# Attention and a maxout MLP as one hand-ordered pipeline over units of two chunks

## The chip, the cores and the metric

The kernel runs on one core of one Trainium2 chip. The metric is device microseconds of one execution. A core has a matrix engine (PE, with weight loads shown apart as PEld), a vector engine (DVE), an activation engine (ACT), GpSimd (POOL), and SyncE (SP), whose queue here issues all transfers between device memory (DRAM) and the on-chip memory (SBUF). Matmul results land in the accumulators (PSUM), which DVE and ACT read.

## The reference

The inputs r, k, v, w have the shape [4 batches, 8 heads, 768 positions, 48]; w is a decay between 0.8 and 0.95. For each batch and head a 48x48 state runs over the positions, and its outputs, put together over the heads, are 3072 tokens of 384 features for a maxout MLP:

```
for t in range(S):
    cur = u * k[t] outer v[t]
    y[t] = r[t] @ (state + cur)
    state = w[t][:, None] * state + k[t] outer v[t]
x = y as [3072 tokens, 384]
out = np.maximum(x @ w1, x @ w2) @ w_out        # w1, w2: [384, 1024], w_out: [1024, 384]
```

The result is f32.

## The kernel before, in words

Positions are cut into chunks of 128, so that a batch has 6 chunks and the whole has 24, taken batch by batch (L98 to L188). For a chunk the decays are summed as logarithms: `lw` is the logarithm of w (ACT, L116), a matmul with a triangle of ones gives the sum over the earlier positions, `excl_p` (L118), and two exponentials give the factors by which r and k are scaled (`Aexcl`, `Ainv`). The scaled `rp` and `kp` are transposed head by head on PE, 48 columns each (L153, L154), and copied out of PSUM by DVE (`rT`, `kT`). Scores `mt_p` are one matmul a head (L163), are masked by DVE (`MTm`, L164), and give `y_p` with v (L168) and with the state of the chunk before (L171). The term with u is a DVE reduction (`diag`) times v. The state `S_new` gets k transposed times v (L180) and is scaled by the decay of the whole chunk, `Wtot_b`: eight matmuls a chunk against a column of ones (L141) put the sum of `lw` over the chunk onto the partitions that hold the state's rows, and ACT takes the exponential (L143). All chunk outputs go to `x_sb`, which stays on chip.

The MLP starts when the attention has ended, in 6 blocks of 512 tokens. max(a, b) is taken as (a + b + |a - b|) / 2: `wd_sb` is w1 - w2, `gT` is the absolute value of x @ wd (L210, L212), and the half that is linear in x is one matmul with `wc_sb` = (w1 + w2) @ w_out, made before the attention (L82 to L91). Tokens are transposed to feature-major `xT` (L204, L205); the result `op` is feature-major too (L216, L219), is copied (L222), transposed back on PE (L225), copied by DVE (L227) and stored in 64 KB pieces (L229).

Every engine works through its instructions in order. The order is set by the framework's scheduler, which takes the program as written and moves instructions of each engine ahead by its own costs; waits between engines are semaphores that the framework puts in. A tile of a pool with one buffer (all PSUM tiles but `mt_p`) is written again only when its last reader is done.

## Time and profile before

| | before |
|---|---|
| three timed runs, median (lowest to highest) | 425.43 us (425.3 to 425.91) |
| profiled execution: its span, first to last instruction | 422.0 us |
| the same execution with what lies around the span, 3.4 us by the median of the timed runs | 425.4 us |
| attention with its preparation, up to about | 300 us |
| MLP, from about | 300 us to 422 us |
| busy: PE, DVE, ACT, POOL | 314.5, 244.0, 142.7, 2.7 us |
| mean granted TensorE clock | 0.687 of full speed |

How to read the views: a row of the groups has the source line, the engine, the operation, the tile written and the tiles read, shapes and count, then busy microseconds in total, the mean of one in nanoseconds, and the idle time of the engine just before with what ended it. A row of the timeline has the start, the duration from the first to the end of the last instruction of the row, the engine (SPq is the queue of SP: the time that it spends on issuing a transfer, not the transfer) and the instruction, with xN for N of a kind. A matmul with f32 operands is two instructions in every view. A matmul's own duration includes its way through the array; a row of several gives the spacing, which is what N of them cost in a stream. A row of the stages has start and end, length, busy time and count of each engine, the granted clock of TensorE (1.00 is full speed, 0.50 half), the mean busy share of the DMA engines, and GB/s.

### The profile page before, as it was taken

The page shows a single profiled execution, that of the slowest core. Times are in us where ns is not written, and L with a number is a line of the kernel's source. Part 1 is how long each engine was busy: PE and PEld are TensorE (multiplying, and loading weights), DVE is VectorE, ACT ScalarE, POOL GpSimd, SP SyncE. Part 2 cuts the span into 40 slices and gives each one's busy share as a digit, 9 for nine tenths or more (in the row PEclk, how much of TensorE's full clock was granted, in tenths as well). Part 3 has the DMA queues.
Part 4 walks back from the last instruction along what each step waited for, and adds up shares of the span by engine and source line. Part 5 has one row for each costly group of instructions (what it writes and reads, how often), then busy time and mean ns, then how long its engine had stood idle before and what let it go on. Part 6 is the DMA issues. An engine that isn't in the chain of part 4 may idle for free.

```text
span 422.0 us, 5555 instructions
## 1 busy us (share of the span) xinstructions
PE 314.5 (75%) x2078; PEld 189.2 (45%) x2088; DVE 244.0 (58%) x596; ACT 142.7 (34%) x206; POOL 2.7 (1%) x16
## 2 busy tenths in 40 slices
...
PEclk9998565555555555555555555555799999999997
...
DMA packets 112076, 28.67 MB, mean 68 GB/s; under 512 B 101041, under 2 KB 111282, under 8 KB 112050
## 3 DMA queue, kind: packets, MB, share of 16 engines
...
## 4 chain that ended last, share of the span: by engine, by line
PE 53%; DVE 18%; ACT 17%; DMA 6%; issue 5%; SPq 0%; ACTq 0%; DVEq 0%
PE g L210 9%; PE Wtot_p L141 7%; PE y_p L168 6%; ACT gT L212 6%; PE y_p L171 6%; PE op L216 5%; ACT L116 5%; PE tp_k L154 5%; DVE MTm L164 4%; PE mt_p L163 3%; DVE x_sb L175 3%; PE op L219 3%; PE tp_r L153 3%; DVE S_new L184 2%; DMA w2f<-in_moe_w_dram 2%
## 5 line engine op out<-in xcount | busy, mean ns | idle before, releaser
L118 PE MATMUL excl_p<-lw,triU 128*128 128x384 f32 x48 | 38.8, 910 | 34.2 <-DVE incl L122 33.5
L143 ACT ACTIVATE Wtot_b<-Wtot_p 48x384 f32<-48x384 f32 x24 | 11.6, 484 | 120.8 <-DVE S_new L184 119.6
L210 PE MATMUL g<-xT,wd_sb 128*128 128x512 bf16 x138 | 41.4, 391 | 13.5 <-ACT gT L212 12.4
L205 DVE COPY xT<-tp 128x128 bf16<-128x128 bf16 x72 | 16.1, 224 | 54.0 <-PE tp L204 54.0
L212 ACT ACTIVATE gT<-g 128x512 bf16<-128x512 f32 x48 | 28.7, 597 | 53.5 <-PE g L210 52.7
L216 PE MATMUL op<-gT,wo_sb 128*128 128x512 bf16 x140 | 41.6, 381 | 3.8 <-ACT gT L212 2.5
L227 DVE CAST osx<-tp 128x128 f32<-128x128 bf16 x72 | 20.8, 289 | 40.7 <-PE tp L225 27.6
L168 PE MATMUL y_p<-vb,MTm 128*128 128x48 bf16 x192 | 38.1, 220 | 5.7 <-DVE MTm L164 5.7
L141 PE MATMUL Wtot_p<-ones_col,lw 128*48 128x1 f32 x384 | 33.2, 216 | 5.2 <-ACT lw L116 3.5
L141 PEld LDWEIGHTS Wtot_p<-ones_col,lw 128*48 128x48 f32 x384 | 31.2, 186 | 10.5 <-ACT lw L116 7.8
L171 PE MATMUL y_p<-S_b_new,rT 48*128 48x48 bf16 x160 | 34.8, 218 | 0.0
L156 DVE COPY kT<-tp_k 48x512 bf16<-48x512 bf16 x48 | 19.9, 414 | 23.2 <-PE tp_k L154 23.1
L164 DVE TENSOR_TENSOR MTm<-mt_p,maskU 128x512 bf16<-128x512 f32 x48 | 31.0, 686 | 2.7 <-PE mt_p L163 0.2
L153 PE MATMUL tp_r<-ident,rp 128*48 128x128 bf16 x192 | 29.8, 308 | 2.8 <-DVE rp L127 2.5
L153 PEld LDWEIGHTS <-rp 128*48 128x48 bf16 x192 | 18.3, 145 | 26.9 <-DVE vb L131 16.2
L154 PE MATMUL tp_k<-ident,kp 128*48 128x128 bf16 x192 | 29.8, 309 | 0.7 <-DVE kT L156 0.4
L163 PE MATMUL mt_p<-rT,kT 48*128 48x128 bf16 x192 | 28.3, 302 | 0.5 <-DVE kT L156 0.5
L116 ACT ACT_TABLE_LOAD x22 | 28.2, 1283 | 1.1 <-PEq L248 0.7
L118 PEld LDWEIGHTS excl_p<-lw,triU 128*128 128x128 f32 x48 | 11.8, 305 | 37.0 <-DVE incl L122 35.8
L120 ACT ACT_TABLE_LOAD x22 | 28.2, 1283 | 0.4
L210 PEld LDWEIGHTS <-wd_sb 128*128 128x128 bf16 x144 | 13.9, 98 | 31.7 <-issue 22.8
L168 PEld LDWEIGHTS <-MTm 128*128 128x128 bf16 x192 | 18.4, 106 | 19.3 <-DVE MTm L164 12.5
...
## 6 DMA issues: line engine op xcount, KB each, us to landing
rt<-in_r_dram SPq DMA_DIRECT2D x24, 192.0 KB, 3.8
kt<-in_k_dram SPq DMA_DIRECT2D x24, 192.0 KB, 3.6
vt<-in_v_dram SPq DMA_DIRECT2D x24, 192.0 KB, 2.7
wt<-in_w_dram SPq DMA_DIRECT2D x24, 192.0 KB, 3.1
out_dram<-osx SPq DMA_DIRECT2D x72, 64.0 KB, 1.5
w1f<-in_moe_w_dram SPq DMA_DIRECT2D x1, 1536.0 KB, 6.4
w2f<-in_moe_w_dram SPq DMA_DIRECT2D x1, 1536.0 KB, 9.9
wof<-in_moe_w_out_dram SPq DMA_DIRECT2D x1, 1536.0 KB, 7.1
```

What stands on the lines that cost most here:

```text
L116: nc.scalar.activation(lw, wt, AF.Ln)
L118: nc.tensor.matmul(excl_p, triU, lw.rearrange("a b c -> a (b c)"))
L141: nc.tensor.matmul(Wtot_p[:, h:h + 1], lw[:, h, :], ones_col)
L153: nc.tensor.transpose(tp_r[:, j, :], rp[:, h, :], ident)
L154: nc.tensor.transpose(tp_k[:, j, :], kp[:, h, :], ident)
L163: nc.tensor.matmul(mt_p[:, j, :], kT[:, h, :], rT[:, h, :])
L164: nc.vector.tensor_mul(MTm[:, half * 4:half * 4 + 4, :], mt_p, maskU4)
L168: nc.tensor.matmul(y_p[:, h * D:(h + 1) * D], MTm[:, h, :], vb[:, h, :], start=True, stop=(c == 0))
L171: nc.tensor.matmul(y_p[:, h * D:(h + 1) * D], rT[:, h, :], S_b[:, h, :], start=False, stop=True)
L210: nc.tensor.matmul(g1, wd_sb[:, ko, fo * C:(fo + 1) * C], xT[:, ko, :], start=(ko == 0), stop=(ko == KO - 1))
L212: nc.scalar.activation(gT[:, fo, :], g1, AF.Abs)
L216: nc.tensor.matmul(op, wo_sb[:, fo, ko * C:(ko + 1) * C], gT[:, fo, :], start=(fo == 0), stop=False)
```

## The change

The function is written anew. The work is cut into 12 units; a unit is one chunk position of two batches (J = 2), so that units 2c and 2c + 1 hold chunk c of batches 0, 1 and 2, 3. The framework's scheduler is off (`manual_schedule`): each engine does its instructions in the order of the code. A loop of 14 steps takes in step n three units at different stages, interleaved piece by piece: unit a = n is prepared (decay sums `cs`, scaling `pre3`), unit t = n - 1 is in the attention proper (`tr`, `qk`, `kv`, `yy`, `decay`, and `xt`, the transpose of its outputs), and unit m = n - 2 is in the MLP (`gg`, `oo`).

Inside the pieces:

- Loads are 384 KB each, four a unit, issued two steps ahead. The MLP weights are loaded behind the inputs of units 0 and 1, and made ready (`weights`) in step 1.
- One table of ACT functions that holds both logarithm and exponential is loaded once.
- r and k of a head lie in 64 columns of which 16 are zero, so that one transpose takes two heads (8 transposes of 128 columns a chunk, for r and k together, where there were 16), and the second head's rows start at partition 64.
- The decay of a whole chunk comes from the last row of the inclusive sums `inc`: a transfer writes this row to DRAM, two transfers read it back one element at a time onto the partitions of the state (`WL`), and ACT takes the exponential (`Wt`). The matmuls against the column of ones are gone.
- The copy of v, the product with u, its product with v, and the state's scaling and copy go from DVE to POOL.
- The state's matmul and its use take two heads at once, with zero blocks beside the diagonal ones.
- The MLP's second product is token-major: `xT` and `gT` are the weights and `wo_sb`, `wc_sb` stream with 384 columns. The result is copied by ACT and stored, 192 KB a chunk, with no transpose back. The factor 0.5 sits in `wo_sb`, which ACT makes.
- PSUM tiles: one buffer each for `ex`, `tr`, `sc0`, `sc1`, `y`, `o`, two for `g`. `tr` serves `tr` and `xt`, `ex` serves `cs` and `kv`.

The diff, added lines only; the lines it takes away are the kernel above:

```diff
+    with tc.manual_schedule(), nc.allow_non_contiguous_dma(reason="one row moved onto partitions"):
+        _body(tc, r, k, v, w, u, moe_w1, moe_w2, moe_w_out, out)
...
+    NP = H // 2
+    J = 2
+    DP = 64
+    NU = NC * B // J
+    nc.scalar.preload_act_table_set("natural_log_exp_and_others")
     const = tc.alloc_tile_pool(name="cst", bufs=1)
+    ldp = tc.alloc_tile_pool(name="ld", bufs=4)
+    wk = tc.alloc_tile_pool(name="wk", bufs=2)
+    drp = tc.alloc_tile_pool(name="dr", bufs=3, space=bass.MemoryType.DRAM)
+    ps = tc.alloc_tile_pool(name="ps", bufs=1, space=bass.MemoryType.PSUM)
+    def unit(u_):
+        return u_ // 2, (u_ % 2) * J
+    L = {}
+    def load(u_):
+        c, b0 = unit(u_)
+        sl = bass.ds(c * C, C)
+        d = {}
+        for name, src in (("w", w), ("k", k), ("r", r), ("v", v)):
+            t = ldp.tile([C, J, H, D], F32, tag="l" + name, name="l" + name)
+            nc.sync.dma_start(
+                out=t.rearrange("s b h d -> s (b h) d"),
+                in_=src[b0:b0 + J, :, sl, :].rearrange("b h s d -> s (b h) d"))
+            d[name] = t
+        L[u_] = d
+    load(0)
+    u_b = const.tile([C, HD], F32)
+    nc.sync.dma_start(out=u_b, in_=u.rearrange("h d -> (h d)").partition_broadcast(C))
+    load(1)
+    w1f = const.tile([C, KO, d_ff], F32)
+    w2f = const.tile([C, KO, d_ff], F32)
+    wof = const.tile([C, FO, HD], F32)
+    nc.sync.dma_start(out=w1f, in_=moe_w1.rearrange("(o p) n -> p o n", p=C))
+    nc.sync.dma_start(out=w2f, in_=moe_w2.rearrange("(o p) n -> p o n", p=C))
+    nc.sync.dma_start(out=wof, in_=moe_w_out.rearrange("(o p) n -> p o n", p=C))
...
+    def weights():
+        for ko in range(KO):
+            nc.vector.tensor_sub(wd_sb[:, ko, :], w1f[:, ko, :], w2f[:, ko, :])
+            nc.gpsimd.tensor_add(ws_sb[:, ko, :], w1f[:, ko, :], w2f[:, ko, :])
+        nc.scalar.mul(wo_sb, wof, 0.5)
...
+        for ko in range(KO):
+            wc_p = ps.tile([C, HD], F32, tag="o", name="o")
+            for fo in range(FO):
+                nc.tensor.matmul(wc_p, wsT_sb[:, fo, ko * C:(ko + 1) * C],
+                                 wo_sb[:, fo, :], start=(fo == 0), stop=(fo == FO - 1))
+            nc.scalar.copy(wc_sb[:, ko, :], wc_p)
+    U = {}
+    def pre1(n):
+        t = L[n]
+        s = {}
+        U[n] = s
+        s["lw"] = lw = wk.tile([C, J, H, D], F32, tag="lw", name="lw")
+        nc.scalar.activation(lw, t["w"], AF.Ln)
+        s["vb"] = vb = wk.tile([C, J, H, D], BF16, tag="vb", name="vb", bufs=3)
+        nc.gpsimd.tensor_copy(vb, t["v"])
+        rku = wk.tile([C, J, H, D], F32, tag="rku", name="rku", bufs=1)
+        nc.gpsimd.tensor_mul(rku, t["r"], t["k"])
+        nc.gpsimd.tensor_mul(
+            rku.rearrange("s j h d -> s j (h d)"), rku.rearrange("s j h d -> s j (h d)"),
+            u_b.unsqueeze(1).to_broadcast([C, J, HD]))
+        s["rku"] = rku
+        s["inc"] = wk.tile([C, J, HD], F32, tag="inc", name="inc")
+        s["A"] = wk.tile([C, J, H, D], F32, tag="A", name="A")
+    def pre1b(n):
+        s = U[n]
+        dg = wk.tile([C, J, H, 1], F32, tag="dg", name="dg")
+        nc.vector.reduce_sum(dg, s["rku"], axis=AX.X)
+        s["vd"] = vd = wk.tile([C, J, H, D], F32, tag="vd", name="vd", bufs=3)
+        nc.gpsimd.tensor_mul(vd, L[n]["v"], dg.to_broadcast([C, J, H, D]))
+    def cs(n, j):
+        s = U[n]
+        ex = ps.tile([C, HD], F32, tag="ex", name="ex")
+        nc.tensor.matmul(ex, triU, s["lw"][:, j].rearrange("s h d -> s (h d)"))
+        nc.scalar.activation(s["A"][:, j].rearrange("s h d -> s (h d)"), ex, AF.Exp)
+        nc.vector.tensor_add(s["inc"][:, j, :], ex, s["lw"][:, j].rearrange("s h d -> s (h d)"))
+    def pre3(n):
+        s = U[n]
+        iA = wk.tile([C, J, H, D], F32, tag="iA", name="iA", bufs=1)
+        nc.scalar.activation(iA.rearrange("s j h d -> s j (h d)"), s["inc"], AF.Exp, scale=-1.0)
+        s["WL"] = wl = WL[n % NW]
+        row = drp.tile([J * HD], F32, tag="row", name="row")
+        nc.sync.dma_start(out=row.unsqueeze(0), in_=s["inc"][C - 1:C].rearrange("o j x -> o (j x)"))
+        rowv = row.rearrange("(q r d) -> r d q", r=2, d=D)
+        for par in range(2):
+            nc.sync.dma_start(
+                out=wl[par * DP:par * DP + D, :, :].rearrange("d j p -> d (j p)"),
+                in_=rowv[par])
+        s["Wt"] = wt = wk.tile([C, J, NP], F32, tag="Wt", name="Wt")
+        nc.scalar.activation(wt, wl, AF.Exp)
+        rkn = rkn_b[n % NRK]
+        s["rkn"] = rkn
+        for j in range(J):
+            nc.vector.tensor_mul(rkn[:, j, 0, :, 0:D], L[n]["r"][:, j], s["A"][:, j])
+            nc.vector.tensor_mul(rkn[:, j, 1, :, 0:D], L[n]["k"][:, j], iA[:, j])
+    def tr(n, j):
+        s = U[n]
+        tp = ps.tile([C, 2 * NP, C], BF16, tag="tr", name="tr")
+        for q in range(2 * NP):
+            nc.tensor.transpose(
+                tp[:, q, :],
+                s["rkn"][:, j].rearrange("s x (p r) d -> s (x p) (r d)", r=2)[:, q, :], ident)
+        rkT = wk.tile([C, 2 * NP, C], BF16, tag="rkT", name="rkT", bufs=3)
+        s["rkT", j] = rkT
+        nc.vector.tensor_copy(rkT, tp)
+    def qk(n, j):
+        s = U[n]
+        rkT = s["rkT", j]
+        sc = [ps.tile([C, NP, C], F32, tag=f"sc{e}", name=f"sc{e}") for e in range(2)]
+        for p in range(NP):
+            for e in range(2):
+                nc.tensor.matmul(sc[e][:, p, :], rkT[e * DP:e * DP + D, NP + p, :],
+                                 rkT[e * DP:e * DP + D, p, :])
+        M = wk.tile([C, 2, NP, C], BF16, tag="M", name="M")
+        s["M", j] = M
+        for e in range(2):
+            nc.vector.tensor_mul(M[:, e], sc[e], maskU)
+    def kv(n, j):
+        c, b0 = unit(n)
+        b = b0 + j
+        if c == NC - 1:
+            return
+        s = U[n]
+        kp = ps.tile([C, NP, 2 * D], F32, tag="ex", name="ex")
+        for p in range(NP):
+            nc.tensor.matmul(kp[:, p, :],
+                             s["rkn"][:, j, 1, 2 * p:2 * p + 2, :].rearrange("s r d -> s (r d)"),
+                             s["vb"][:, j, 2 * p:2 * p + 2, :].rearrange("s r d -> s (r d)"),
+                             start=(p == 0), stop=(p == NP - 1), skip_group_check=True)
+        for e in range(2):
+            q = slice(e * DP, (e + 1) * DP)
+            nc.vector.tensor_add(T_f[b][q], kp[q, :, e * D:(e + 1) * D], S_f[b][q])
+    def decay(n, j):
+        c, b0 = unit(n)
+        b = b0 + j
+        if c == NC - 1:
+            return
+        wt = U[n]["Wt"]
+        wbc = wt[:, j, :].unsqueeze(2).to_broadcast([C, NP, D])
+        nc.gpsimd.tensor_mul(S_f[b], T_f[b], wbc)
+        for e in range(2):
+            q = slice(e * DP, (e + 1) * DP)
+            nc.gpsimd.tensor_copy(S_b[b][q, :, e * D:(e + 1) * D], S_f[b][q])
+    def yy(n, j):
+        c, b0 = unit(n)
+        b = b0 + j
+        s = U[n]
+        y = ps.tile([C, HD], F32, tag="y", name="y")
+        first = True
+        if c > 0:
+            for p in range(NP):
+                nc.tensor.matmul(y[:, p * 2 * D:(p + 1) * 2 * D], s["rkT", j][:, p, :],
+                                 S_b[b][:, p, :], start=first, stop=False, skip_group_check=True)
+                first = False
+        for e in range(2):
+            for p in range(NP):
+                h = 2 * p + e
+                nc.tensor.matmul(y[:, h * D:(h + 1) * D], s["M", j][:, e, p, :],
+                                 s["vb"][:, j, h, :], start=first,
+                                 stop=(e == 1 and p == NP - 1), skip_group_check=True)
+                first = False
+        x = wk.tile([C, HD], BF16, tag="x", name="x")
+        s["x", j] = x
+        nc.vector.tensor_add(x, y, s["vd"][:, j].rearrange("s h d -> s (h d)"))
+    def xt(n, j):
+        s = U[n]
+        if j == 0:
+            s["xT"] = wk.tile([C, KO, J, C], BF16, tag="xT", name="xT", bufs=3)
+        tp = ps.tile([C, KO, C], BF16, tag="tr", name="tr")
+        for ko in range(KO):
+            nc.tensor.transpose(tp[:, ko, :], s["x", j][:, ko * C:(ko + 1) * C], ident)
+        nc.scalar.copy(s["xT"][:, :, j, :], tp)
+    def gg(n, q):
+        s = U[n]
+        if q == 0:
+            s["gT"] = wk.tile([C, FO, J * C], BF16, tag="gT", name="gT")
+        g = ps.tile([C, 2, J * C], F32, tag="g", name="g", bufs=2)
+        for f in range(2):
+            fo = 2 * q + f
             for ko in range(KO):
+                nc.tensor.matmul(g[:, f, :], wd_sb[:, ko, fo * C:(fo + 1) * C],
+                                 s["xT"][:, ko].rearrange("p j t -> p (j t)"),
+                                 start=(f == 0 and ko == 0), stop=(f == 1 and ko == KO - 1),
+                                 skip_group_check=True)
+        nc.scalar.activation(s["gT"][:, 2 * q:2 * q + 2, :], g, AF.Abs)
+    def oo(n, j, part=None):
+        c, b0 = unit(n)
+        s = U[n]
+        if part in (None, 0):
+            s["o", j] = ps.tile([C, HD], F32, tag="o", name="o")
             for ko in range(KO):
+                nc.tensor.matmul(s["o", j], s["xT"][:, ko, j, :], wc_sb[:, ko, :],
+                                 start=(ko == 0), stop=False)
+        lo, hi = {None: (0, FO), 0: (0, 3), 1: (3, FO)}[part]
+        o = s["o", j]
+        for fo in range(lo, hi):
+            nc.tensor.matmul(o, s["gT"][:, fo, j * C:(j + 1) * C], wo_sb[:, fo, :],
+                             start=False, stop=(fo == FO - 1))
+        if part in (None, 1):
+            osb = wk.tile([C, HD], F32, tag="osb", name="osb", bufs=3)
+            nc.scalar.copy(osb, o)
+            tok = (b0 + j) * S + c * C
+            nc.sync.dma_start(out=out[tok:tok + C, :], in_=osb)
+    pre1(0)
+    pre1b(0)
+    for n in range(NU + 2):
+        a, t, m = n, n - 1, n - 2
+        A, T, M = a < NU, 0 <= t < NU, 0 <= m < NU
+        if n + 2 < NU:
+            load(n + 2)
+        if n == 1:
+            weights()
+        if A: cs(a, 0)
+        if T: tr(t, 0)
+        if M: gg(m, 0)
+        if A: cs(a, 1)
+        if a + 1 < NU: pre1(a + 1)
+        if T: qk(t, 0)
+        if M: gg(m, 1)
+        if T: tr(t, 1)
+        if T: kv(t, 0)
+        if M: gg(m, 2)
+        if T: yy(t, 0); decay(t, 0)
+        if A: pre3(a)
+        if T: qk(t, 1)
+        if M: gg(m, 3)
+        if T: xt(t, 0)
+        if M: oo(m, 0)
+        if T: kv(t, 1)
+        if T: yy(t, 1); decay(t, 1)
+        if a + 1 < NU: pre1b(a + 1)
+        if M: oo(m, 1)
+        if T: xt(t, 1)
...
```

How this moves instructions, at three places. First SP at the program's start, where the loads stand. Before, the weights w1 and w2 and then one chunk's inputs (rt, kt, vt, wt) were first:

```order
L55 DMA u_small<-in_u_dram 1x384
L63 DMA w1f<-in_moe_w_dram 128x3x1024
L65 DMA w2f<-in_moe_w_dram 128x3x1024
L110 DMA rt<-in_r_dram 128x8x48
L111 DMA kt<-in_k_dram 128x8x48
L112 DMA vt<-in_v_dram 128x8x48
L113 DMA wt<-in_w_dram 128x8x48
```

Now, behind the four loads of unit 0, u, and the four of unit 1, stand the weights, then the loads of unit 2, and only then the row of unit 0 (`row`, `WL`):

```order
L82 DMA w1f<-in_moe_w_dram 128x3x1024
L83 DMA w2f<-in_moe_w_dram 128x3x1024
L84 DMA wof<-in_moe_w_out_dram 128x8x384
L69 DMA lw<-in_w_dram 128x16x48
L69 DMA lk<-in_k_dram 128x16x48
L69 DMA lr<-in_r_dram 128x16x48
L69 DMA lv<-in_v_dram 128x16x48
L178 DMA row<-inc 1x768
L181 DMA WL_139<-row 48x8x1 x2
```

The weights moved from the front to behind two units' inputs, and a transfer that needs computed data stands behind three units' inputs.

Second, SP in the middle of the program. Before, the loads of the last chunks were followed by all the stores:

```order
L111 DMA kt<-in_k_dram 128x8x48
L110 DMA rt<-in_r_dram 128x8x48
L112 DMA vt<-in_v_dram 128x8x48
L229 DMA out_dram<-osx 128x128 x72
```

Now each step has the two stores of the unit in the MLP, then the loads of a unit, then the row of the unit being prepared:

```order
L306 DMA out_dram<-osb 128x384 x2
L69 DMA lw<-in_w_dram 128x16x48
L69 DMA lk<-in_k_dram 128x16x48
L69 DMA lr<-in_r_dram 128x16x48
L69 DMA lv<-in_v_dram 128x16x48
L178 DMA row<-inc 1x768
L181 DMA WL_140<-row 48x8x1 x2
```

The stores now stand ahead of loads, and the loads ahead of the row.

Third, ACT in one round. Before, a chunk's round had two table loads:

```order
L125 ACTIVATE Ainv<-incl 128x384
L116 ACT_TABLE_LOAD
L116 ACTIVATE lw<-wt 128x384
L120 ACT_TABLE_LOAD
L120 ACTIVATE Aexcl<-excl_p 128x384
L143 ACTIVATE Wtot_b<-Wtot_p 48x384
```

Now a step's round, for two chunks, has none, and holds the MLP's work too; `Wt`, which waits for the row, stands ahead of the last `gT` (`A`, `iA` are the two exponentials; `osb` the copies of the result):

```order
L169 ACTIVATE A<-ex 128x384
L287 ACTIVATE gT<-g 128x512
L169 ACTIVATE A<-ex 128x384
L146 ACTIVATE lw<-lw 128x768
L287 ACTIVATE gT<-g 128x512 x2
L175 ACTIVATE iA<-inc 128x768
L185 ACTIVATE Wt<-WL_140 128x8
L287 ACTIVATE gT<-g 128x512
L273 COPY xT<-tr 128x3x128
L304 COPY osb<-o 128x384 x2
L273 COPY xT<-tr 128x3x128
```

Between the third `gT` and the last one of a unit an instruction moved in that waits for a transfer. In the first rounds the same holds of `wo_sb`, the weight of the second product, which stands behind the `Wt` of unit 0.

204 lines of the change are left out of this document (35 added, 169 removed).

## The prediction

> **What bounds the kernel now.** I read the page first: busy shares, the granted clock, and the chain of waits.
>
> ```profile
> span 422.0 us, 5555 instructions
> PE 314.5 (75%) x2078; PEld 189.2 (45%) x2088; DVE 244.0 (58%) x596; ACT 142.7 (34%) x206; POOL 2.7 (1%) x16
> ...
> PEclk9998565555555555555555555555799999999997
> ...
> PE 53%; DVE 18%; ACT 17%; DMA 6%; issue 5%; SPq 0%; ACTq 0%; DVEq 0%
> ```
>
> No engine is full, and the chain goes through all of them: PE 53%, DVE 18%, ACT 17%. That is a kernel bound by the waits between its stages, with PE as the slowest part. The view by stages says why PE is slow.
>
> ```profile
> 31.92:38.75 6.83, 4.87 (x47) 3.11 (x46) 2.14 (x4) 1.13 (x3) 0.00 (x0) 0.98 0.56 74
> 55.80:59.20 3.40, 2.91 (x29) 2.22 (x29) 2.27 (x5) 0.59 (x2) 0.00 (x0) 0.97 0.17 34
> 59.20:301.60 242.40, 191.59 (x1396) 127.01 (x1397) 180.06 (x413) 85.45 (x117) 0.00 (x0) 0.50 0.31 59
> 301.60:417.60 116.00, 90.60 (x451) 41.33 (x458) 31.20 (x127) 38.07 (x64) 0.00 (x0) 1.00 0.14 40
> 332.05:335.46 3.41, 2.01 (x12) 0.88 (x10) 1.04 (x5) 0.60 (x1) 0.00 (x0) 1.00 0.09 23
> ```
>
> The attention (59.20 to 301.60, with the MLP's first microsecond) runs at half clock with PE busy 79% of the time, the MLP (301.60 to 417.60) at full clock with 78%. So what counts for the clock is not busy time: the attention's matmuls are narrow (48 to 128 columns), those of the MLP 512 wide. Full clock came in stretches of 3.4 us or multiples, and fell back after the stretch at 55.80, with nothing but narrow matmuls. The stretch at 332.05 kept it with PE busy for 2.01 of 3.41 us.
>
> The Trainium skill, "TensorE: Matmul & The Clock Gate" (Part 1), has the rule behind it: half or full clock, decided on windows of 3.4 us by how busy the array was. The rows agree: 3.40 and 6.83 us long.
>
> **The change part by part.** First what leaves.
>
> ```profile
> L116 ACT ACT_TABLE_LOAD x22 | 28.2, 1283 | 1.1 <-PEq L248 0.7
> L141 PE MATMUL Wtot_p<-ones_col,lw 128*48 128x1 f32 x384 | 33.2, 216 | 5.2 <-ACT lw L116 3.5 <-ACT Wtot_b L143 1.7
> ```
>
> All 44 table loads but one go (22 here, as many at L120, 56 us of ACT), and the matmuls for the chunk's decay (33.2 us of PE). Neither is subtracted as such, since the order is new: I add up the new kernel instead, engine by engine and then along its waits. A "step" is one round of the loop, for two chunks.
>
> *DVE, ACT and POOL in a step*, from these groups and their slopes:
>
> ```profile
> L122 DVE TENSOR_TENSOR incl<-excl_p,lw 128x384 f32<-128x384 f32 x24 | 12.9, 537 | 3.6 <-ACT Aexcl L120 3.6
> L127 DVE TENSOR_TENSOR rp<-rt,Aexcl 128x384 bf16<-128x384 f32 x24 | 13.0, 543 | 0.0
> L137 DVE TENSOR_REDUCE diag<-uk 128x8 f32<-128x384 f32 x24 | 12.9, 536 | 0.1
> L164 DVE TENSOR_TENSOR MTm<-mt_p,maskU 128x512 bf16<-128x512 f32 x48 | 31.0, 686 | 2.7 <-PE mt_p L163 0.2
> L175 DVE TENSOR_TENSOR x_sb<-x_sb,y_p 128x384 bf16<-128x384 bf16 x24 | 13.2, 552 | 22.1 <-PE y_p L171 22.1
> L83 DVE COPY wsT_sb<-tp 128x1024 bf16<-128x1024 bf16 x3 | 2.1, 687 | 0.0
> L116 ACT ACTIVATE lw<-wt 128x384 f32<-128x384 f32 x24 | 12.5, 522 | 26.7 <-DMA wt<-in_w_dram 26.5
> L120 ACT ACTIVATE Aexcl<-excl_p 128x384 f32<-128x384 f32 x24 | 11.8, 491 | 7.7 <-PE excl_p L118 7.4
> L212 ACT ACTIVATE gT<-g 128x512 bf16<-128x512 f32 x48 | 28.7, 597 | 53.5 <-PE g L210 52.7
> masks.py:66 POOL TENSOR_SCALAR_AFFINE_SELECT maskU<-maskU 128x128 f32<-128x128 f32 x4 | 1.1, 302 | 0.0
> L248 POOL MEMSET const-float32-1.0<- 128x1 f32 x1 | 0.1, 99 | 0.0
> ```
>
> DVE: 2 inc (0.54), 4 scalings (0.54), 4 masks of 512 (0.69), 2 sums x (0.55), 2 copies of 1024 out of PSUM (0.69), one reduction of 768 (0.54 and 384 more elements at 1.16 ns, (686 - 537) / 128: 0.98) and four additions of 64x192 (0.54 less 192 elements: 0.32): 10.7 us. *ACT*, at 0.83 ns an element ((597 - 491) / 128): 6 operations of 384 (0.49), 4 of 512 (0.60), 2 of 768 (0.84), and the small Wt (0.2): 7.2 us. *POOL* does arithmetic on wide tiles that no row shows. Its nearest row is 302 ns for 128 elements; 99 ns of it is start (a memset of one element takes that), so 1.6 ns an element: with four operations of 768, two of 192 and four half-wide ones of 192 that is 7.7 us a step, and 12 if a second input doubles it. Three engines thus fit below PE.
>
> *PE in a step.* The rows of the timeline that price it, at full clock (33.22 to 35.42, 56.08 to 58.59, 315.17) and at half (the others):
>
> ```profile
> 27.21 2.72 PE L89 MATMUL wc_p<-wo_sb,wsT_sb 128*128 128x384 bf16 x8 [3.83 <-DVE wo_sb L70]
> 33.22 1.46 PE L89 MATMUL wc_p<-wo_sb,wsT_sb 128*128 128x384 bf16 x8 [0.65 <-DVE wc_sb L91]
> 35.42 0.88 PE L118 MATMUL excl_p<-lw,triU 128*128 128x384 f32 x2 [0.74 <-DVE wc_sb L91]
> ...
> 56.08 0.39 PE L163 MATMUL mt_p<-rT,kT 48*128 48x128 bf16 x4 [0.28 <-DVE kT L156]
> 56.68 0.20 PE L168 MATMUL y_p<-vb,MTm 128*128 128x48 bf16 x1 [0.20 <-DVE MTm L164]
> 58.59 0.19 PE L171 MATMUL y_p<-S_b_new,rT 48*128 48x48 bf16 x1
> 61.50 1.65 PE L118 MATMUL excl_p<-lw,triU 128*128 128x384 f32 x2
> ...
> 101.79 0.62 PE L153 MATMUL tp_r<-ident,rp 128*48 128x128 bf16 x4
> ...
> 315.17 1.46 PE L216 MATMUL op<-gT,wo_sb 128*128 128x512 bf16 x6
> ```
>
> At full clock 384 columns are spaced 0.165 us ((1.46 - 0.3) / 7) and 512 are 0.216, so 256 are 0.108; a narrow matmul with 128 weight columns 0.127 (16 from 56.68 to 58.59); a score matmul 0.06; a transpose between 0.06 and the 0.103 of half clock. So: decay sums 2 x 0.88 = 1.7; 22 transposes 2.0; 24 of gg 2.6; 16 scores 1.3; 8 of kv 0.8; 24 of yy 3.0; 22 of oo 3.6: 15.0, and 18 pieces that each wait some 0.13 for their operands or drain: **17.3 us**. At half clock (1.65, 0.103, 0.216, 0.10, 0.10, 0.15, 0.33 in the same order): 24.1 + 2.3 = **26.4 us**.
>
> *The new wait.* The decay now takes the way inc, row to DRAM, WL back, Wt on ACT. On SP the row stands behind four loads of 384 KB, and these behind the stores of the step before. What a load costs there, by SP's rows of the timeline:
>
> ```profile
> 1.14 0.41 SPq L63 DMA_DIRECT2D w1f<-in_moe_w_dram  x1
> 1.60 0.47 SPq L65 DMA_DIRECT2D w2f<-in_moe_w_dram  x1
> 12.10 1.00 SPq L110 DMA_DIRECT2D rt<-in_r_dram  x1
> 13.14 1.00 SPq L111 DMA_DIRECT2D kt<-in_k_dram  x1
> ...
> 102.58 0.37 SPq L113 DMA_DIRECT2D wt<-in_w_dram  x1
> 103.67 0.74 SPq L110 DMA_DIRECT2D rt<-in_r_dram  x1
> ```
>
> and, from the page's list of transfers, size and median time from issue to landing:
>
> ```profile
> rt<-in_r_dram SPq DMA_DIRECT2D x24, 192.0 KB, 3.8
> out_dram<-osx SPq DMA_DIRECT2D x72, 64.0 KB, 1.5
> w2f<-in_moe_w_dram SPq DMA_DIRECT2D x1, 1536.0 KB, 9.9
> ```
>
> Loads that follow each other come 1.04 us apart for 192 KB. At 102.58 three start, and the last is there 3.8 us after its issue at 103.67, 4.9 us in all: 3 x 1.04 and 1.8 to get going. SP hands over a load quickly only while the queue has room (0.37, then 0.74); with 8.3 us of loads in each step it stands until nearly all are through. Let t = 0 be the end of the second osb of a step, which frees SP to go on:
>
> - store issued and loads begun by 0.5; loads through at 0.5 + 1.8 + 8.3 + 0.5 (the store's share) = 11.1; the row lands behind them at 11.6 (bounds 0.1 and the store's 1.5 after the loads);
> - SP wakes and issues two WL, 0.9; they land 1.7 later (bounds 1.5 of a store, 3.8 of a load): 14.2;
> - Wt, and behind it on ACT the last gT of this step: 0.3 + 0.7, so 15.2;
> - PE has meanwhile done the step's first part (about 11.3 us at full clock) and waits in oo for this gT; then two matmuls, kv, yy, eleven of oo and osb: 0.5 + 0.4 + 1.6 + 2.0 + 0.5 = 5.0, or 7.3 at half clock.
>
> That closes a circle of 20.2 to 22.5 us, longer than PE's 17.3. The PE wait of nearly 4 us is as long as a clock stretch, so I expect about a third of what follows it at half clock, and take **21.0**. Behind the waiting Wt stand gT, xT and osb on ACT; for these wait PE, and for osb SP.
>
> The Trainium skill ("TensorE: Matmul & The Clock Gate", Part 4) has a rule against the change: transposes do not count as PE activity for the full clock. 22 of the 118 matmuls of a step are such. No row here separates it. By it the clock would drop more often, the circle be 22.5 throughout, and the time 296 + 7 x 1.5 = 306.
>
> *The start.* Order on the queue: unit 0, u, unit 1, weights, unit 2, row of unit 0. From 0.7 + 1.8, three units at 8.3, u 0.5, and weights 12.8 (w1 and w2 together 11.5 - 1.1 - 1.8 = 8.5; the third, half as many bytes, 4.3) make 40.7. Row, WL and Wt bring 45.0. On ACT wo_sb stands behind this Wt: 3072 elements, 2.7, to 47.7; the wc products in three groups with copies took 8.1 before (27.2 to 35.3): **55.8**. PE has all of the attention behind them in order. Step 1 follows DVE (inc, copy, masks, x, scalings, masks, x with their waits, about 12.3): 68.1. Step 2 (17.3, less the state's eight of yy, 1.0, plus 2.1 for a start at half clock) 18.4: **86.5**.
>
> *The sum.* Steps 3 to 9 load: 7 x 21.0 = 147.0, to 233.5. Steps 10 and 11 have no loads, so the row is early and PE sets 17.3: 268.1. Step 12 (no preparation, no state) 14.5, step 13 (MLP alone) 7.8, last store and end 2.4 (1.5 to land): span 292.8. With the 3.4 us around it **296 us**, against 422.0 + 3.4 = 425.4 of the profiled execution, which is the median of the runs.
>
> **The rivals.**
>
> 1. *The row is early enough*: the loads leave SP free sooner, or the row passes them. Then PE's 17.3 sets steps 3 to 9: 296 - 7 x 3.7 = 270. For it: the issue at 103.67 took only 0.74. Against: issues of 1.00 where loads follow each other at 12.10.
> 2. *Half clock throughout*, as in the attention before. Steps 2 to 11 at 26.4, the first part as above, 22 and 13 for the last steps: 68 + 264 + 35 + 2.4 + 3.4 = 373. For it: 70 of a step's 118 matmuls are narrow. Against: half of PE's time is 256 and 384 wide, and wide ones at half clock raised it at 301.60.
> 3. *The reading back of the row is slow*, the one way to the other side: 768 elements of 4 bytes, one packet each. A load's 1024 packets over 16 engines in 1.04 us are 16 ns a packet on one engine. If all 768 fall on one engine, WL takes 12.3 us more, in each of steps 1 to 11, of which steps 2, 10 and 11 can absorb a part: 414. It is slower than before from about 17.5 ns a packet, and at 20 ns near 445. For it: nothing here has ever read single elements. Against: 48 partitions are as easily spread as 128.
> 4. *An order that stalls elsewhere* (POOL at its upper bound or more, single PSUM buffers), costing 2 to 4 us more a step in 11 steps: 320 to 340.
>
> **How the numbers follow.** The forecast, with steps set by the row, 278 to 318, has 0.54. Rival 1, 255 to 278, 0.23; rival 2, 345 to 390, 0.09; rival 3 0.04, of it 0.03 slower than before; rival 4 0.10. The time is that of the forecast, 296; the range 258 to 342 takes in the forecast, most of rival 1 and rival 4. A measurement here tells 0.2% from no change. Faster 0.96; within 0.2%, 0.01; slower 0.03.
>
> **What would show it.** In the changed profile, steps of about 21 us, on PE a wait of 3 to 4 us before the last two matmuls of the first oo (by ACT gT), on ACT one before Wt by a transfer, and SP issuing loads for some 7 us a step. wo_sb starts near 45 us and the first decay sums of step 1 near 56. The last two steps with preparation are 3 to 4 us shorter. Clock mostly 1.00 after about 75 us with single stretches of 0.50. Wrong if steps are equally long with and without loads, if PE waits for DVE or POOL, or if the first step begins before 45.

## Result: 255.0 us, with steps set by the row's way as forecast, but all of them shorter

| | before | after |
|---|---|---|
| median of the timed runs | 425.37 us | 255.0 us |
| lowest to highest, 4 runs each | 422.54 to 425.91 | 254.66 to 256.86 |
| profiled execution: time, span | 425.4, 422.0 | 255.22, 253.3 |

The ratio is 0.601, 95% interval 0.598 to 0.604: faster by 40%. The forecast was 296 us with a range of 258 to 342, so the time lies 3 us below its lower end. One run of all those below, 215.1 us of the kernel with the row ahead of the loads, was slow (1.8% above the fastest run of that kernel) and is left out of its figures.

The page of the changed kernel, busy shares, clock and the chain of waits:

```profile
span 253.3 us, 3818 instructions
...
PE 163.0 (64%) x1456; PEld 106.3 (42%) x1456; DVE 135.8 (54%) x242; ACT 84.1 (33%) x161; POOL 110.8 (44%) x123
...
PEclk9999999995799979979899679799689779999999
...
PE 31%; DMA 21%; DVE 19%; ACT 9%; SPq 8%; issue 7%; POOL 3%; ACTq 0%; POOLq 0%; DVEq 0%
DMA row<-inc 10%; PE o L300 10%; DMA WL<-row 6%; SPq L69 6%; DVE M L214 5%; PE ex L168 4%; PE g L283 4%; DMA w2f<-in_moe_w_dram 4%; PE o L295 4%; DVE Tf L230 3%; DVE wd_sb L122 3%; PE tr L196 2%; DVE rkT L201 2%; ACT A L169 2%; ACT osb L304
```

The clock is now 0.91 in the mean. The chain goes through "DMA row<-inc" (10%) and "DMA WL<-row" (6%), transfers of 3 KB: the way of the row, which the prediction had made the bound of the steps. The list of waits names the same place:

```profile
ACT Wt L185 <- DMA WL<-row: 73.3, 12, 20.3
...
PE o L300 <- ACT gT L287: 34.5, 7, 5.5
```

12 waits of ACT for WL, and 7 of PE for gT ahead of the last two matmuls of the first oo: one in each of the steps 3 to 9, the last seven that load, 4.9 us on average and 5.5 at most. One such step on ACT and on SP's queue, from one second osb to the next (columns: start, duration, engine, operation, and in brackets the idle time ahead with its releaser):

```profile
76.07 0.48 ACT L304 COPY osb<-o 128x384 f32<-128x384 f32 x1 [2.83 <-PE o L300]
...
89.24 0.21 ACT L185 ACTIVATE Wt<-WL 128x8 f32<-128x8 f32 x1 [6.52 <-DMA WL<-row]
...
94.53 0.48 ACT L304 COPY osb<-o 128x384 f32<-128x384 f32 x1 [3.38 <-PE o L300]
```

```profile
76.98 0.43 SPq L69 DMA_DIRECT2D lw<-in_w_dram  x1
77.50 2.52 SPq L69 DMA_DIRECT2D lk<-in_k_dram  x1
80.07 1.45 SPq L69 DMA_DIRECT2D lr<-in_r_dram  x1
81.57 1.51 SPq L69 DMA_DIRECT2D lv<-in_v_dram  x1
83.18 1.31 SPq L178 DMA_DIRECT2D row<-inc  x1
86.79 0.85 SPq L181 DMA_DIRECT2D WL<-row  x2
```

SP issues loads until 83.1, then the row, and goes on with WL at 86.8, since WL waits until the row has landed. Wt starts at 89.24: 12.7 us after the end of the second osb. Windows of the same step, cut at Wt, and of step 10, the first without loads (columns: length, busy time of PE, PEld, DVE, ACT, POOL, granted clock, DMA share, GB/s):

```profile
76.55:89.24 12.69, 8.05 (x88) 5.38 (x85) 8.05 (x15) 4.51 (x9) 7.06 (x7) 1.00 0.76 141
89.24:95.01 5.77, 5.03 (x34) 3.15 (x35) 2.13 (x4) 2.02 (x6) 2.88 (x5) 0.70 0.12 37
...
205.77:218.67 12.90, 12.08 (x124) 8.10 (x122) 10.09 (x19) 6.52 (x13) 6.75 (x9) 0.98 0.12 33
```

Up to Wt the clock is full and PE is busy for 8 of 12.7 us; behind it, after PE has stood for 5.0 us, it falls to 0.70. Step 10 has the same computation in 12.9 us. From second osb to second osb, steps 3 to 9 take 17.2 to 19.7 us, on average (205.77 - 76.07) / 7 = 18.53: 12.56 up to Wt and 5.97 from there. Steps 10 to 13 take 12.9, 11.6, 10.6 and 8.3.

### The profile page after: what moved, and what is told of

It is laid out like the page before. It is cut to its first block, busy times and chain, and to the rows that moved or that the text cites. A ratio compares the mean times of both kernels' runs of the same rounds, so it can differ in the third digit from the quotient of the medians.

```text
span 253.3 us, 3818 instructions
## 1 busy us (share of the span) xinstructions
PE 163.0 (64%) x1456; PEld 106.3 (42%) x1456; DVE 135.8 (54%) x242; ACT 84.1 (33%) x161; POOL 110.8 (44%) x123
## 4 chain that ended last, share of the span: by engine, by line
PE 31%; DMA 21%; DVE 19%; ACT 9%; SPq 8%; issue 7%; POOL 3%; ACTq 0%; POOLq 0%; DVEq 0%
DMA row<-inc 10%; PE o L300 10%; DMA WL<-row 6%; SPq L69 6%; DVE M L214 5%; PE ex L168 4%; PE g L283 4%; DMA w2f<-in_moe_w_dram 4%; PE o L295 4%; DVE Tf L230 3%; DVE wd_sb L122 3%; PE tr L196 2%; DVE rkT L201 2%; ACT A L169 2%; ACT osb L304 2%
## 5 line engine op out<-in xcount | busy, mean ns | idle before, releaser
L300 PE MATMUL o<-wo_sb,gT 128*128 128x384 bf16 x192 | 43.4, 369 | 34.6 <-ACT gT L287 34.5
L239 POOL TENSOR_TENSOR Sf<-Tf,Wt 128x192 f32<-128x192 f32 x20 | 10.1, 505 | 91.6 <-DVE Tf L230 91.6
L300 PEld LDWEIGHTS <-gT 128*128 128x128 bf16 x192 | 20.0, 108 | 53.3 <-ACT gT L287 38.0
L283 PE MATMUL g<-xT,wd_sb 128*128 128x256 bf16 x288 | 39.8, 276 | 0.9 <-ACT xT L273 0.8
L168 PE MATMUL ex<-lw,triU 128*128 128x384 f32 x48 | 23.9, 583 | 15.1 <-DVE inc L170 9.5
L214 DVE TENSOR_TENSOR M<-sc,maskU 128x512 bf16<-128x512 f32 x48 | 30.7, 679 | 0.5 <-PE sc L209 0.5
L185 ACT ACTIVATE Wt<-WL 128x8 f32<-128x8 f32 x12 | 2.5, 208 | 73.3 <-DMA WL<-row 73.3
L151 POOL TENSOR_TENSOR rku<-rku,u_b 128x768 f32<-128x768 f32 x12 | 21.9, 1829 | 0.9
L150 POOL TENSOR_TENSOR rku<-lr,lk 128x768 f32<-128x768 f32 x12 | 22.0, 1834 | 0.0
L163 POOL TENSOR_TENSOR vd<-lv,dg 128x768 f32<-128x768 f32 x12 | 17.7, 1473 | 4.4 <-DVE dg L161 4.4
L295 PE MATMUL o<-wc_sb,xT 128*128 128x384 bf16 x72 | 19.0, 381 | 0.9 <-ACT osb L304 0.9
L242 POOL CAST Sb<-Sf 64x192 bf16<-64x192 f32 x40 | 18.1, 453 | 2.1
(43 smaller groups left out, 220.6 us busy)
```

The costliest lines, as they stand in the source:

```text
L150: nc.gpsimd.tensor_mul(rku, t["r"], t["k"])
L151: nc.gpsimd.tensor_mul(rku.rearrange("s j h d -> s j (h d)"), rku.rearrange("s j h d -> s j (h d)"), u_b.unsqueeze(1).to_broadcast([C, J, ...
L168: nc.tensor.matmul(ex, triU, s["lw"][:, j].rearrange("s h d -> s (h d)"))
L214: nc.vector.tensor_mul(M[:, e], sc[e], maskU)
L242: nc.gpsimd.tensor_copy(S_b[b][q, :, e * D:(e + 1) * D], S_f[b][q])
L283: nc.tensor.matmul(g[:, f, :], wd_sb[:, ko, fo * C:(fo + 1) * C], s["xT"][:, ko].rearrange("p j t -> p (j t)"), start=(f == 0 and ko == 0) ...
```

## Experiments

The theory C is the circle of the prediction: stores, then loads, then row and WL on SP; then Wt, and behind it the last gT, on ACT; then oo and osb, which let SP go on. "Step" below is the mean of steps 3 to 9, by the starts of the second osb.

### The row ahead of the loads

```
 in the loop:
-        if n + 2 < NU: load(n + 2)        # at its head
         ...
         if A: pre3(a)
+        if n + 2 < NU: load(n + 2)
```

> Edit: the loads of unit n+2 are issued on SP behind the row and WL of unit n, no longer ahead of them; nothing else moves. Theory C (the circle through SP: loads ahead of the row, Wt ahead of the last gT on ACT) says that steps 3 to 9, now 18.5 us on average, fall to what the steps without loads take, 12.9 us (step 10 of the changed kernel): 7 x 5.6 = 39 us, so 255 - 39 = 216 us, 210 to 224. The wait of ACT for WL ahead of Wt falls from about 7 us a step to under 2. Rival R (steps 3 to 9 are long because 1.7 MB a step has to come in beside the work, or because an engine needs that long; the wait for Wt only covers it) says the wait moves to another place, at least 240 us.

**211.9 us** (211.3 to 212.4; ratio to before 0.499, 0.497 to 0.501), as expected. A step is 13.2 us. The wait of PE for gT is down from 34.5 to 0.4 us in all:

```profile
PE o L300 <- ACT gT L287: 0.4, 1, 0.4
```

Nothing was taken out, and 43 us went with the order of the issues. Some 5 of them are the start (second osb of step 2 at 70.9 instead of 76.1), where the row of unit 0 now also comes ahead of load 2; the rest are the steps.

### Wt behind oo, SP as it was

```
 pre3:   -        nc.scalar.activation(wt, wl, AF.Exp)      # and wt's tile
 loop:            if T: xt(t, 1)
         +        if A: decay_factors(a)                    # Wt of unit a
```

> Edit: the order on SP stays; the Wt activation of unit a stands at the end of its step on ACT, behind the last gT, xT and both osb, instead of ahead of the last gT. Theory C says that the row may then come as late as it likes, since only the next step's decay on POOL needs Wt: steps 3 to 9 fall to about 13 us, 216 us in all (210 to 226). If the SP queue alone makes the circle (the stores of osb stand behind WL, whose issue waits for the row), SP is busy for some 10.5 us a step, still below PE's 12.9, and the result is the same. Rival R: at least 240 us. If the decay on POOL is what really needs the row in time, this kernel stays near 255 while the one with the row ahead of the loads falls.

**213.5 us** (212.7 to 214.2), as expected. Here the row is as late as before, and it does not matter. The circle needs both of its links, the row behind the loads and the last gT behind Wt, and opening either ends it. That the two times are so close is in part chance: this kernel's step is 0.5 us shorter (12.72), but its second osb of step 2 comes at 75.4, 4.5 us later. The steady step (windows, columns as above):

```profile
101.41:114.02 12.61, 11.55 (x123) 7.89 (x122) 10.09 (x19) 6.43 (x14) 8.65 (x10) 1.00 0.84 158
```

12.61 us, and within 0.02 us the same in steps 3 and 5 to 9 (step 4 took 13.40), at full clock, with PE busy for 11.55 of it. This is what the computation takes in this order when no transfer is in the way, the number that the prediction had put at 17.3.

### One more load, and two less, ahead of the row

```
 e4:  +    extra(n + 2)            # 384 KB of v into a tile of its own, behind load(n + 2)
 e8:       load(n + 2, 0)          # head of the step: only w and k
           ...
           if A: pre3(a)
      +    if n + 2 < NU: load(n + 2, 1)      # r and v
```

> Edit: each step loads one tile more (384 KB of v, into a tile that nothing reads), behind its four loads and ahead of the row. Theory C: every byte ahead of the row is on the path; a load of 384 KB takes 1.45 to 1.5 us on SP in the changed kernel, so steps 2 to 9 take 1.5 us more each and the start 1.5: 8 x 1.5 + 1.5 = 13.5, so 268 us (264 to 272). By my prediction's price for a load (1.04 us per 192 KB) it would be 9 x 2.1 = 19, 274 us. Rival R with an engine as the bound: within 3 us of 255.

**269.9 us** (268.4 to 270.5), 15 more than the changed kernel and as expected. A step is 20.31 us, 1.78 more. From the end of the second osb to Wt it is 14.22 on average (12.56 in the changed kernel), the rest stays: 6.09 against 5.97. So a load of 384 KB ahead of the row costs 1.66 us of the way there.

> Edit: of the four loads a step, two (w and k) stay ahead of the row on SP, two (r and v) go behind it and WL. Theory C, dose and response: one load more ahead of the row made a step 1.78 us longer (20.31 against 18.53 us), all four behind it 5.7 us shorter (12.6 to 13). So two less ahead: 18.5 - 2 x 1.78 = 15.0 us for steps 3 to 9, which is still above the 12.6 that the engines need: 255 - 7 x 3.5 = 230 us, and up to 4 less from the start, 224 to 234. If the order alone counts and not the bytes (a row that stands behind any load is late): above 245; if the wait was already gone with two: 212 to 218.

**211.1 us** (210.5 to 211.9): as good as with all four behind the row, and not the 230 expected. A step is 13.14. One of its steps on ACT:

```profile
97.35 0.48 ACT L304 COPY osb<-o 128x384 f32<-128x384 f32 x1 [2.36 <-PE o L300]
...
106.54 0.21 ACT L185 ACTIVATE Wt<-WL 128x8 f32<-128x8 f32 x1 [2.59 <-DMA WL<-row]
...
110.38 0.48 ACT L304 COPY osb<-o 128x384 f32<-128x384 f32 x1 [2.08 <-DMA lv<-in_v_dram]
```

(The releaser in the last line is the one that the profile saw last; PE's own matmuls for this osb end at 110.30 too.) On average Wt starts 8.50 us after the end of the second osb, 4.06 earlier than in the changed kernel, and the tail from Wt to the end of the next second osb is 4.64 instead of 5.97.

Both parts broke my straight line. First, 4.06 us is not the price of two loads. In the step shown SP is through with w and k at 100.30 and then stands until `inc` is there: the second `inc` ends on DVE at 101.34, and the row is issued at 101.37. The loads ahead of it no longer decide when the row goes out; the row still takes 2.7 us from there until SP goes on with WL, against 1.2 with no loads ahead of it. Second, PE waits 1.07 us ahead of its last two matmuls here, 0.86 on average, instead of 4.9, and the tail got shorter by itself. That this is the clock is shown by one of the seven steps, in which PE waited 1.78 us. From Wt to the end of the second osb, in the step above and in the one behind it (columns as above):

```profile
106.54:110.86 4.32, 3.54 (x34) 2.41 (x35) 3.32 (x6) 2.02 (x6) 1.74 (x4) 1.00 1.01 215
120.28:126.28 6.00, 5.22 (x34) 2.96 (x35) 2.61 (x5) 2.02 (x6) 3.42 (x6) 0.72 0.67 142
```

The same 34 matmuls take 3.54 us at full clock and 5.22 at 0.72, and this step took 15.42 us, where the other six took 12.58 to 13.09. Those six are already at the 12.6 of the kernel with Wt behind oo, so taking the last two loads away brought nothing more. The wait was worth more than its length: it took clock from the work behind it. Its length alone does not decide: with the row ahead of the loads, a wait of PE of 2.17 us in step 3 left the clock at 1.00.

### The weights one step later

```
-        if n == 1: weights()
+        if n == 2: weights()
```

> Edit: the preparation of the MLP's weights (wd, ws, wo, wsT, wc) stands at the head of step 2 instead of step 1, on all engines; no transfer moves. In the changed kernel step 1 begins at 49.7 us, since its decay sums stand behind the wc products on PE. Theory S (the order alone holds step 1 back): step 1 runs while weights are still on their way, up to where its decay waits for Wt of unit 0 at 39.9, and the preparation, some 10 us from Wt to the last wc copy, moves behind it: 5 to 10 us less, 247 us (243 to 251). Rival D (the start is bound by bytes: 8.6 MB until unit 2 is there): no change, 253 to 257, since the step then waits for the same transfers.

**261.2 us** (260.9 to 262.3), 6 us slower than the changed kernel: both expectations failed. Step 1 on ACT, and ws on POOL:

```profile
39.53 0.21 ACT L185 ACTIVATE Wt<-WL 128x8 f32<-128x8 f32 x1 [20.15 <-DMA WL<-row]
39.64 0.47 ACT L169 ACTIVATE A<-ex 128x384 f32<-128x384 f32 x1
...
52.10 2.77 ACT L124 ACTIVATE wo_sb<-wof 128x3072 bf16<-128x3072 f32 x1
```

```profile
54.41 8.90 POOL L123 TENSOR_TENSOR ws_sb<-w1f,w2f 128x1024 bf16<-128x1024 f32 x3
```

The first exponential A of step 1 stands behind Wt of unit 0 on ACT, and so step 1 begins at 39.6 whatever the weights do. The subtractions and additions for wd and ws, which in the changed kernel ran between 26.8 and 36.8 while ACT waited for the row, are now done later, at 52 to 63, with ACT and PE waiting for them. In the changed kernel:

```profile
26.84 9.95 POOL L123 TENSOR_TENSOR ws_sb<-w1f,w2f 128x1024 bf16<-128x1024 f32 x3 [0.56 <-DMA w2f<-in_moe_w_dram]
```

The work took nearly as long (8.90 us on POOL against 9.95); it lost its cover.

### Table loads back, with and without the wait

```
-    nc.scalar.preload_act_table_set("natural_log_exp_and_others")
```

> Edit: the preloaded table of ACT is left out, one part of the change undone: 24 table loads come back, two a step, each 1.28 us, one ahead of Ln (lw) and one ahead of the Exp for iA; the rest is the changed kernel. Theory C (steps 3 to 9 wait some 7 us for WL on ACT right behind iA): there the loads fall into that wait and cost nothing or little; they show only in the start (2 or 3 of them) and in steps 2, 10 and 11: 255 + 6 us, 258 to 264. Rival T, on which each load lies on the path: 24 x 1.28 = 31, 283 to 288 us.

**255.25 us** (254.9 to 256.2), the changed kernel's time, and less than the 258 to 264 expected. Its groups on ACT:

```profile
L146 ACT ACT_TABLE_LOAD x12 | 15.4, 1283 | 0.9 <-PEq L359 0.7
L175 ACT ACT_TABLE_LOAD x11 | 14.1, 1283 | 0.2
...
L185 ACT ACTIVATE Wt<-WL 128x8 f32<-128x8 f32 x12 | 2.5, 206 | 46.5 <-DMA WL<-row 46.5
```

With one more for A these are 24 loads, 31 us of ACT, and 27 of them have come out of the wait for WL: it is 46.5 us in all, against 73.3.

> Edit: the same table loads come back, but in the kernel whose Wt stands behind oo (213.5 us), so without the wait on ACT. ACT then has 12.6 us a step and 7 us of work; with 2.6 more it is still not full. If a table load only costs where ACT has no wait to put it in: up to 22 x 1.28 = 28 us, since A, lw and iA feed DVE and PE within the step; by half of it 227 us (218 to 241). If the slack of ACT (12.6 less 9.6 us) covers it: within 4 us of 213.5. Both this and the run without the move of Wt together tell whether the price of the table loads depends on the row's wait.

**222.2 us** (221.4 to 222.8; 218 to 241 expected), 8.7 more than the same kernel with the preloaded table, and a step of 13.65 instead of 12.72. So two table loads of 1.28 us cost 0.9 us a step where ACT has no wait to hide them in, and nothing where it has. The preloaded table, the easiest saving to see in the profile before, brings the changed kernel nothing that can be measured; it begins to pay once the circle is open.

### The pipeline undone

```
     for n in range(NU):
         cs(n, 0); cs(n, 1); pre1(n + 1); pre3(n); load(n + 2)
         tr(n, 0); qk(n, 0); ...; xt(n, 1)
         for q in range(4): gg(n, q)
         oo(n, 0); oo(n, 1)
```

> Edit: from the kernel with the row ahead of the loads (212 us), the pipeline is undone: one round does decay sums, scores, state, transposes, gg and oo of the same unit, one behind the other, instead of the three stages of units n, n-1 and n-2 interleaved. The operations are the same. Theory: each piece waits for the one before it through DVE and ACT, PE falls below what keeps its clock, and one unit takes some 31 us by the rows (at half clock: decay sums and their exponentials 4.5, iA 0.8, scalings 2.6, transposes, scores, masks, y and x of both chunks 9, gg 5.8, oo 7.8); 27 to 31 for 12 units behind a start of 30 to 45: 380 us (340 to 410), clock near 0.6 in the mean. Rival: the clock is set by the amount of work alone, and stays high: under 310 us.

**327.0 us** (two runs, 326.3 and 327.7), between the two expectations.

Three windows of one unit: decay sums to the first scores, the rest of the attention, gg and oo (columns as above):

```profile
181.84:191.00 9.16, 4.60 (x44) 2.89 (x42) 5.37 (x10) 3.13 (x6) 0.00 (x0) 0.82 0.37 73
191.00:196.00 5.00, 2.89 (x37) 2.18 (x34) 4.60 (x10) 0.96 (x2) 2.54 (x7) 0.50 1.24 221
196.00:205.70 9.70, 9.13 (x47) 5.89 (x47) 0.00 (x0) 2.87 (x5) 5.64 (x4) 0.72 0.07 23
```

A unit takes 23.9 us, less than the 27 to 31 expected: the clock does not stay down. It falls to 0.50 in the middle of the attention, comes back during the wide gg and oo, and lasts into the next unit; 0.76 in the mean. Compared with 211.9 us, the same operations with the stages interleaved, the overlap is worth 115 us (the weights are made ready in the first round here, so a little of this can be the start). The other 97 us, from 424 to 327, lie in what else the change does (fewer and other operations, the MLP's matmuls right behind each unit's attention); they were not taken apart further.

### The start, and who disturbs whom

Two kernels then changed the start: unit 0's Wt and decays go behind step 1, its row ahead of load 2; ws from POOL to DVE; the weights behind step 1, and their transposes and products inside step 2. g1 is built on the kernel with Wt behind oo (the transposes and products ahead of the last gg, in the others behind the decay sums) and moves, beside that, the decays of every step to its end; g2 leaves these in the middle; g4 is g2 with the decays at the end, and g3 is g2 with a copy moved.

```
 g1, g4:  +   if T: ...; decay(t, 0); decay(t, 1)        # at the end of the step
 g2:          if T: yy(t, 0)
              if t > 0 and T: decay(t, 0)                # in the middle, as before
 all:     +   nc.vector.tensor_add(ws_sb[:, ko, :], ...)  # was nc.gpsimd
          +   if n == 1: weights(); pre1(2)              # behind xt(t, 1)
          +   if n == 2: weights2()                      # transposes and wc products
 g3:      +   rkT of j = 1: nc.scalar.copy(rkT, tp)      # was nc.vector.tensor_copy
```

> Edit: from the kernel with Wt behind oo (213.5 us): Wt of unit t and both decays go to the end of step t+1, where nothing waits for them until step t+2; the row of unit 0 is issued ahead of load 2; pre1b(0) comes behind the decay sums; ws_sb goes from POOL to DVE, wd and ws, wo and the preparation of unit 2 stand behind step 1, and the transposes and wc products ahead of the last gg of step 2. Theory from the start of the earlier runs (step 1 stood behind Wt of unit 0 on ACT at 39.5 us also where the weights were moved, 261.2 us): step 1 now needs only units 0 and 1, which are in by about 17, and ends near 33; weights 33 to 43 on DVE (wd and ws at some 1.15 us a piece without POOL beside it, against 2.3 to 2.7 with it); the second osb of step 2 near 58 instead of 75.4, and the steps behind it at 12.6: 213.5 - 17 = 196 us (190 to 206). Rival (the start is bound by the arrival of the weights and unit 2): 205 to 213.

**220.6 us** (219.4 to 220.6), 7 slower than what it was built from, though nothing waits for the decays, and not the 196 expected. Its second osb of step 2 comes at 73.3 instead of the expected 58, because the last gg of that step now stands behind wsT and wc, and these behind dg of unit 2 and its scalings on DVE; and its steps are 13.83. wd and ws did become fast, as expected: on DVE alone, against the changed kernel's with POOL beside it,

```profile
34.33 3.49 DVE L122 TENSOR_TENSOR wd_sb<-w1f,w2f 128x1024 bf16<-128x1024 f32 x3
37.73 3.49 DVE L124 TENSOR_TENSOR ws_sb<-w1f,w2f 128x1024 bf16<-128x1024 f32 x3
```

```profile
L122 DVE TENSOR_TENSOR wd_sb<-w1f,w2f 128x1024 bf16<-128x1024 f32 x3 | 7.8, 2647 | 2.1 <-DMA w2f<-in_moe_w_dram 2.1
```

1.16 us each instead of 2.65.

> Edit: from the kernel with Wt behind oo (213.5 us): the decays stay in the middle of the step (only unit 0's go to the end of step 1), Wt stands ahead of the decays on ACT; rows of units 0 and 1 are issued ahead of loads 2 and 3; ws_sb on DVE; wd, ws, wo and the preparation of unit 2 behind step 1, transposes and wc products behind the decay sums of step 2. Theory P (POOL and DVE get in each other's way: in the kernel with the decays at the end of the step the multiplication by u on POOL fell on the first scaling of DVE, which took 2.0 us instead of 0.56, and the step 13.8 instead of 12.6): with the decays back, POOL's multiplications run beside DVE's operations out of PSUM again and the steps are 12.6. Start: step 2 ended at 73.3 there because wsT, wc and gg stood in one row behind dg of unit 2 (45.6); now wc is ready near 50 and step 2 ends near 60: 213.5 - 75.4 + 60 = 198 us (193 to 206). If the steps stay at 13.8 the theory on POOL falls: 207 to 217.

**198.0 us** (197.4 to 198.3; ratio to before 0.4665, 0.4652 to 0.4677), as expected, with the second osb of step 2 at 62.1 and a step of 12.59.

> Edit: one thing against g2 (198.0 us): both decays stand at the end of each step on POOL, behind vd, instead of in the middle, so POOL's two multiplications for rku start some 2.6 us later in the step. No operation is added, and the decays are needed only two steps later. Theory P (an operation of DVE with two inputs in SBUF and one of POOL don't run side by side): the second of them falls on the first scaling rkn, which takes 2.0 us instead of 0.56; steps 3 to 10 are 13.8 instead of 12.6: 198 + 8 x 1.2 = 208 us (205 to 211). Rival: the order of POOL, with 8.7 us of work in 12.6, is free: 196 to 200, and the 13.8 in g1 came from something else there.

**209.6 us** (208.1 to 211.0), as expected: 12 more for the place of the two decays on an engine that works 8.7 of 12.6 us. One step each, on DVE and on POOL, first of g4:

```profile
96.44 2.13 DVE L190 TENSOR_TENSOR rkn<-lr,A 128x384 bf16<-128x384 f32 x1
98.50 0.55 DVE L191 TENSOR_TENSOR rkn<-lk,iA 128x384 bf16<-128x384 f32 x1
```

```profile
96.34 1.82 POOL L154 TENSOR_TENSOR rku<-rku,u_b 128x768 f32<-128x768 f32 x1
```

and of g2:

```profile
94.22 0.56 DVE L190 TENSOR_TENSOR rkn<-lr,A 128x384 bf16<-128x384 f32 x1
```

```profile
91.43 1.81 POOL L154 TENSOR_TENSOR rku<-rku,u_b 128x768 f32<-128x768 f32 x1
```

The first scaling on DVE has two inputs in SBUF and takes 0.56 us by itself. In g4 POOL's multiplication began 0.1 us earlier, and the scaling ended 0.4 us after POOL's 98.16. By these times it did not run slowly beside the other operation but waited until that was nearly or quite done (spans on POOL are rough). What hangs on it is the step: the masks M come later by as much, and PE waits 1.59 us for them ahead of yy where it waited 0.31 in g2, which is the 1.27 us between the steps of 13.86 and 12.59. The operations of DVE that read PSUM ran beside POOL undisturbed (in g2 the masks and copies, from 91.2 to 93.0, beside POOL's multiplication from 91.43). The Trainium skill says the same under "SBUF — State Buffer" (SBUF: two separate sides): one pair of ports is shared by DVE and GpSimd as an exclusive lock for the length of an instruction, and a DVE operation with two SBUF inputs contends for it with a GpSimd operation that reads SBUF. The trace agrees, with 2.13 us for 0.56.

In part it was there in an earlier kernel too. With the row ahead of the loads, and so the loads later, the scalings took 807 and 736 ns on average, with Wt behind oo 686 and 658, and the steps were 13.2 and 12.7. The averages with the row ahead of the loads, and the first scaling of its longest step (14.49 us) with what POOL did:

```profile
L189 DVE TENSOR_TENSOR rkn<-lr,A 128x384 bf16<-128x384 f32 x24 | 19.4, 807 | 0.0
L190 DVE TENSOR_TENSOR rkn<-lk,iA 128x384 bf16<-128x384 f32 x24 | 17.7, 736 | 0.3 <-ACT iA L175 0.3
```

```profile
77.84 2.12 DVE L189 TENSOR_TENSOR rkn<-lr,A 128x384 bf16<-128x384 f32 x1
```

```profile
77.73 1.81 POOL L151 TENSOR_TENSOR rku<-rku,u_b 128x768 f32<-128x768 f32 x1
```

> Edit: the kernel g2 (start and decays), and in addition the copy of the transposed heads of each second chunk (128x1024 bf16 out of PSUM, 0.68 us on DVE) goes to ACT. DVE has 10.1 us of a 12.6 us step, PE 11.6, ACT 6.4. Theory V (DVE's order and its waits set the 12.6): 0.5 to 0.7 us less a step, 9 steps: 5 us below g2. Theory E (PE with 11.6 us busy is already nearly the bound, or ACT, in its order, comes later with the copy): within 2 us of g2, or slower.

**195.9 us** (195.7 to 196.7; ratio 0.4621, 0.4609 to 0.4633), the fastest of all: 2.1 us less than g2, between the two theories. The step is 12.22 instead of 12.59, 0.37 us shorter where 0.68 left DVE and came to ACT. It beats the changed kernel by 59 us.

## Why the prediction was right about the place and wrong about the time

Two prices of the prediction failed, not its path: 1.04 us for 192 KB of load, which was 0.83 (1.66 for 384 KB), and 0.08 to 0.127 us for a narrow matmul, which was 0.04 to 0.055. They make the steps, the last steps and the start too long.

**The circle: shown.** Steps 3 to 9 were set by the row behind the loads and by gT behind Wt. Opening the circle at either link gave 211.9 and 213.5 us, one more load in it 270. What the prediction named as its marks is there: PE's wait ahead of the last two matmuls of the first oo (4.9 us on average, forecast 3 to 4), ACT's before Wt, SP issuing loads for 5.5 to 7.1 us a step (forecast 7), single stretches of half clock, and steps without loads that are shorter, by about 6 us instead of 3 to 4.

**Where the 41 us went.** Forecast and profiled execution, term by term:

| term | forecast | measured | difference |
|---|---|---|---|
| end of step 2 | 86.5 | 76.6 | -10 |
| steps 3 to 9 | 7 x 21.0 | 7 x 18.5 | -17 |
| steps 10 and 11 | 2 x 17.3 | 12.9 + 11.6 | -10 |
| step 12 | 14.5 | 10.6 | -4 |
| step 13, end, around the span | 13.6 | 8.3 + 3.6 + 1.9 | 0 |

**The circle's 21.0 was 18.5.** WL was to land 14.2 us after the second osb; Wt starts after 12.56. The term "8.3 us of loads" is the one that failed: 1.04 us per 192 KB was taken from two issues of the profile before, 12.10 and 13.14, of transfers half as large. Here SP is through a unit's loads in about 6 us, and one load of 384 KB more costs 1.66 us on the way to Wt where I had 2.08: for four loads 6.6 instead of 8.3, the whole difference of 1.6. The tail was forecast at 6.8 from Wt's start (1.0 and a value of 5.8 between 5.0 and 7.3) and takes 5.97.

**PE's 17.3 was 12.6.** The wide matmuls and the decay sums were priced right. The narrow ones were not; of step 10, at full clock:

```profile
208.90 0.40 PE L209 MATMUL sc<-rkT 48*128 48x128 bf16 x8
...
209.90 0.61 PE L196 MATMUL tr<-ident,rkn 128*128 128x128 bf16 x8
210.34 0.33 PE L224 MATMUL ex<-vb,rkn 128*128 128x96 bf16 x4
...
211.34 0.36 PE L258 MATMUL y<-vb,M 128*128 128x48 bf16 x8
```

Starts of neighbours give 0.041 us a score matmul (0.33 from 208.90 to the next piece, for 8), 0.055 a transpose and 0.04 for the matmuls of kv and yy. The forecast's sum held 0.08 a score (its own row had given 0.06), 0.09 a transpose, 0.10 in kv and 0.127 in yy. The 0.127 came from 16 matmuls of the profile before over 1.9 us. There two kinds took turns, one with 128 rows of weights and one with 48, with no idle time between them; where a kind stood in a row, the same profile has it far closer, even at half clock:

```profile
57.06 0.19 PE L171 MATMUL y_p<-S_b_new,rT 48*128 48x48 bf16 x1
57.19 0.20 PE L168 MATMUL y_p<-vb,MTm 128*128 128x48 bf16 x1
...
104.30 0.53 PE L180 MATMUL kv_p<-vb,kp 128*48 128x48 bf16 x8
...
107.60 0.34 PE L168 MATMUL y_p<-vb,MTm 128*128 128x48 bf16 x4 [0.25 <-DVE MTm L164]
```

With 0.22 us for a single one at half clock, the rows of 8 and of 4 have a spacing of 0.04. The new kernel's yy has each kind in a row. Why taking turns costs three times as much was not tested. By the spacings here the narrow matmuls of a step take 16 x 0.041 + 22 x 0.055 + 32 x 0.042 = 3.2 us, not 7.1. That is 3.9 of the 4.7 us; the rest is in the 18 pieces at 0.13, which were not taken apart. I had taken the price of an order that the new kernel does not have.

**Rival 1's time was wrong for the same reason.** It said 270 for a row that is early enough. The kernels in which it is early, or may be late, took 211.9 and 213.5, with steps of 13.2 and 12.7. The time of 255, just at the lower edge of rival 1's range (255 to 278), would have looked like rival 1; only the trace tells that it is the forecast with smaller terms.

**The start: 10 us early.** On ACT, the changed kernel:

```profile
39.88 0.21 ACT L185 ACTIVATE Wt<-WL 128x8 f32<-128x8 f32 x1 [20.30 <-DMA WL<-row]
40.00 2.75 ACT L124 ACTIVATE wo_sb<-wof 128x3072 bf16<-128x3072 f32 x1
...
49.61 0.48 ACT L136 CAST wc_sb<-o 128x384 bf16<-128x384 f32 x1 [1.55 <-PE o L134]
```

The order was as forecast: row of unit 0, WL, Wt, wo_sb, wc. Wt is done at 40.1 instead of 45.0; the loads term alone, 12 loads at 1.66 instead of 2.08, makes 5.0 of it; wo_sb took the 2.7 forecast; wc was ready at 50.1, 7.3 later (forecast 8.1). Step 1 then took 11.3 (12.3) and step 2 15.2 (18.4), by PE's terms.

**DVE, ACT and POOL.** DVE needs 10.1 us a step (10.7 forecast), ACT 6.5 (7.2), POOL 8.7 (7.7 to 12). None was the bound in the changed kernel. That POOL and DVE can stop each other was missing; it shows in g4 and in the 2.65 us for a piece of wd.

**Half clock throughout, a slow WL, stalls elsewhere.** The clock was full except behind PE's waits: 1.00 from the second osb to Wt in the windows above, 1.00 in the steps 3 to 9 of the kernel with the row ahead of the loads, and 1.00 from 88.01 to 139.24 in the one with Wt behind oo, though 22 of a step's matmuls are transposes. The 306 us that the prediction worked out from the Trainium skill's rule on transposes ("TensorE: Matmul & The Clock Gate", Part 4) did not come; but the transposes are only about 1.2 of PE's 11.55 us in such a step (22 x 0.055), so no run here tells whether they count. WL takes about 2.4 us from its issue to Wt, with single elements and all: rival 3 had nothing to it. The steps without loads (12.9 against a sum of 17.3) leave no room for rival 4 in the changed kernel; a stall of its kind, POOL against DVE, showed in g1 and g4.
